# Last pair's second layer: three passes over 12-bit words instead of Strassen's float32 products

## The chip, the cores and the metric

The kernel runs on one core of a Trainium2 chip. A core has an engine for matrix products (PE, whose weight loads the profile lists apart as PEld), a vector engine (DVE), a scalar engine for activations (ACT), a general engine (POOL) and a queue that issues most transfers (SP). Each works through its own list of instructions in a fixed order, and they wait for each other by semaphores. Operands lie in SBUF, a memory of 128 partitions; products land in PSUM, eight banks of 128 x 512 float32. The metric is the time of one execution in microseconds (us).

## The reference, cut to what matters

A scan over chunks (a Mamba-2 block) makes `x`, 3072 tokens of 256 features. What follows is a two-layer perceptron, and the change is in its second layer:

```python
n_tokens, d_model, d_ff = (3072, 256, 2048)

def _moe_ref(x, w_in, w_out) -> np.ndarray:
    h = x @ w_in
    alpha = 1.0
    g = np.where(h > 0.0, h, alpha * (np.exp(np.minimum(h, 0.0)) - 1.0))
    return (g @ w_out).astype(np.float32)
```

`w_in` is 256 x 2048 and `w_out` 2048 x 256; everything is float32.

## The kernel before, in words

**Tiles.** The tokens are cut into 12 blocks of 256 (4 batches of 3 groups), numbered n = 0 to 11. The scan works block by block; from block 2 on, the perceptron works on pairs (2,3), (4,5) and so on, 512 tokens wide, named by their first block. The hidden layer is cut into 16 slices of 128 features, m = 0 to 15. A step of the main loop makes one slice of one pair.

**The first layer in words.** PE multiplies float32 exactly in several passes, as two instructions for each product. `l1_words` avoids this: it splits the operands into words of some 12 bits, whose products are exact, and PE takes them in the type `float32r` in one instruction each. For every operand there is a high word (made on ACT by a multiplication with `NEAR` that rounds to the type), a low word, and a mixed word "both". A slice is the sum of three passes: high x high and low x low into one PSUM bank (`high`), both x both into another (`both`). Then `4096 * both + 4095 * high` is the exact product. This is L806 (six instructions of 128 x 512 a step). ACT scales `both` into the tile `e` (L812), DVE adds it to `high` (L818), ACT makes Relu and Exp of it (L824 and L825, `begin_end`), and DVE makes the activation `g` (L832, `end_words`). `end_words` of step k stands on DVE in step k+1, just ahead of that step's L818.

**The second layer by Strassen.** `second(n)` multiplies a pair's `g` with `w_out` in float32. It takes Strassen's seven products (in Winograd's form) over quarters: two halves of d_ff, two blocks of tokens, two halves of the 256 outputs. Each product runs over four chunks of a half, with two products of 128 x 128 a chunk (L927), so 7 x 2 x 8 = 112 for a pair. DVE adds the results up (L904, L979), ACT copies two of them (L939, L964), and POOL makes the sums of `g` that Strassen needs (the helper `sub`, L867). `sum_weights` makes the sums of `w_out` on POOL and DVE (L723); it writes the first of them over a quarter of `w_out` itself. Results gather in the tile `c_sum`, and `store` (L984) sends them out.

**Order.** The program is written in the order in which it runs (`manual_schedule`); each engine's list follows it. In the loop over n = 4, 6, 8, 10 (L1327), step k makes slice k of pair n (`l1_words`), does a part of the scan for the pair ahead while there is one, calls `begin_end`, and then takes three or four pieces of `second(n - 2)` (`l2s`). So pair 8's second layer runs inside pair 10's first. Pair 10 is the last; its second layer stands alone behind the loop, as `second(10, True)` (L1376), with the last product's two token halves stored apart (L907 to L919).

**Memory.** Tiles come from pools; tiles with one tag share a fixed number of buffers, and an instruction that writes a new tile waits for the readers of the old one. Seven PSUM banks are shared by all tiles of tag "a" (`high`, `both`, every second of Strassen's sums), the eighth has the tag "o". `raw` and `att` hold what the scan needs, `conv` the words of `w_in` (tags w64, 11 buffers, and w_in, 9 buffers), `ffn` the activations. When pair 10 starts its first layer, the scan is over.

## Time and profile before

| | |
|---|---|
| time, median of 3 runs (lowest to highest) | 350.66 us (350.28 to 351.12) |
| profiled execution, first to last instruction | 347.9 us |
| PE busy in it | 340.7 us (98%) |
| DVE, ACT, POOL busy | 258.4, 234.1, 218.0 us |
| loop n = 10, first L806 to the end of its last | 271.9 to 317.95 us |
| Strassen's products, the last piece of pair 8 and pair 10 | 317.95 to 344.76 us |
| L927, instructions of 128 x 128 in float32 | 276 ns each on the page |
| L806, instructions of 128 x 512 in words | 392 to 437 ns each on the page |

A duration of a matmul on the page contains the way through the pipeline; how fast they follow each other is seen from their starts. The profiled execution's span and the median of the runs differ by 2.8 us, which lie outside the first and last instruction. A group's row ends with the idle time of its engine just before it and with what ended most of that. In rows in order of time the columns are start, duration, engine, line, operation, tiles (out <- in), shapes and count, and in brackets the idle time and what ended it.

### The profile page before, as it was taken

How to read it: one execution, taken by the hardware profiler on the slowest of the kernel's cores; microseconds unless marked ns; L12 is line 12 of the kernel's file. 1: busy time of each engine (PE TensorE's matmuls, PEld its weight loads, DVE VectorE, ACT ScalarE, POOL GpSimd, SP SyncE). 2: the span in 40 equal slices, each digit the busy share in tenths (PEclk: the TensorE clock that was granted, in tenths of full speed). 3: DMA queues.
4: the chain of work that ended last, by engine and by line, in shares of the span. 5: the costliest groups of instructions: out<-in, count | busy, mean ns of one | idle time of the engine just before them, and what ended most of it. 6: DMA issues, size and time to landing. Idle time of an engine off the chain costs nothing.

```text
span 347.9 us, 9991 instructions
## 1 busy us (share of the span) xinstructions
PE 340.7 (98%) x3934; PEld 299.3 (86%) x3934; DVE 258.4 (74%) x515; ACT 234.1 (67%) x537; POOL 218.0 (63%) x338
## 2 busy tenths in 40 slices
PE   8899999999999999999999999999999999999996
PEld 6579888888788889889889888889988989999996
DVE  3998989889997899876788766778776756665232
ACT  4789989598658988457699457599557366565000
POOL 5654554539999799965296765196855174455760
PEclk9999999999999999999999999999999999999999
DMA  8989969381360610260421160320000100001002
GB/s 144 258 204 220 273 130 266 81 150 44 66 138 2 135 38 12 34 137 4 117 51 30 17 154 4 95 44 0 2 2 5 60 2 1 0 2 55 9 2 62
DMA packets 72728, 26.51 MB, mean 76 GB/s; under 512 B 57768, under 2 KB 67560, under 8 KB 72680
## 3 DMA queue, kind: packets, MB, share of 16 engines
q1 hardware_dynamic: 70360, 25.60, 31.7%
q8 instruction: 31, 0.51, 0.6%
q10 hardware_dynamic: 2320, 0.26, 0.5%
q14 instruction: 17, 0.14, 0.1%
HBM read 22.51 MB, written 3.34 MB: 74 GB/s over the span
## 4 chain that ended last, share of the span: by engine, by line
PE 63%; DVE 11%; ACT 10%; POOL 7%; issue 4%; SPq 2%; DMA 2%; DVEq 0%; POOLq 0%; ACTq 0%
PE ps_o L927 22%; PE ps_h L806 11%; PE ps_h L676 11%; PE ps_o L851 8%; PE ps_w L806 6%; DVE ps_h L818 3%; ACT e L824 3%; POOL g L867 3%; ACT e L825 2%; DMA w<-in_moe_w_in_dram 2%; POOL t L867 2%; DVE M L559 2%; PE ps_y L643 2%; DVE y L780 2%; POOL w L867 1%
## 5 line engine op out<-in xcount | busy, mean ns | idle before, releaser
L927 PEld LDWEIGHTS ps_o<-w_out,g 128*128 128x128 f32 x640 | 78.7, 191 | 5.4 <-ACT p_sum L939 1.2
L927 PE MATMUL ps_o<-w_out,g 128*128 128x128 f32 x640 | 81.2, 276 | 0.7 <-ACT p_sum L939 0.6
L824 ACT ACTIVATE e<-ps_h 128x512 f32<-128x512 f32 x72 | 43.0, 598 | 56.9 <-DVE ps_h L818 56.9
L832 DVE SCALAR_TENSOR_TENSOR g<-e,ps_h 128x512 f32<-128x512 f32 x72 | 49.4, 686 | 35.0 <-ACT e L825 33.4
L867 POOL TENSOR_TENSOR g<-g 128x256 f32<-128x256 f32 x36 | 28.6, 794 | 58.2 <-DVE g L832 58.2
L818 DVE SCALAR_TENSOR_TENSOR ps_h<-ps_h,e 128x512 f32<-128x512 f32 x72 | 50.0, 694 | 11.2 <-ACT e L812 9.0
L806 PE MATMUL ps_w<-y_both,w_words 128*128 128x512 f32 x144 | 51.5, 437 | 0.1
L812 ACT ACTIVATE e<-ps_w 128x512 f32<-128x512 f32 x72 | 42.2, 586 | 11.1 <-PE ps_w L806 11.0
L825 ACT ACTIVATE e<-e 128x512 f32<-128x512 f32 x72 | 45.5, 631 | 2.3
L676 PE MATMUL ps_h<-yT,w_in 128*128 128x256 f32 (+1 forms) x208 | 45.1, 367 | 1.9 <-ACT w_in L205 1.1
L806 PE MATMUL ps_h<-y,w_words 128*128 128x512 f32 x144 | 45.5, 398 | 0.0
L806 PE MATMUL ps_h<-y,w 128*128 128x512 f32 x144 | 44.9, 392 | 0.0
L676 PEld LDWEIGHTS ps_h<-yT,w_in 128*128 128x128 f32 x208 | 36.4, 190 | 7.5 <-POOL w_in L248 2.6
L530 ACT ACTIVATE L<-L,ncum 128x64 f32<-128x64 f32 x160 | 42.2, 337 | 0.1
L927 PE MATMUL ps_o<-w_sum,g 128*128 128x128 f32 x304 | 38.6, 276 | 0.0
L927 PEld LDWEIGHTS ps_o<-w_sum,g 128*128 128x128 f32 x304 | 37.0, 192 | 1.4
L535 POOL TENSOR_SCALAR_AFFINE_SELECT L<-L 64x512 f32<-64x512 f32 x40 | 29.4, 735 | 8.0 <-ACT L L530 6.7
L806 PEld LDWEIGHTS ps_h<-y,w 128*128 128x128 f32 x144 | 27.0, 188 | 6.9 <-POOL w L867 0.4
L806 PEld LDWEIGHTS ps_h<-y,w_words 128*128 128x128 f32 x144 | 26.6, 188 | 6.2 <-issue 0.5
L867 POOL TENSOR_TENSOR g<-t,g 128x256 f32<-128x256 f32 x40 | 28.1, 736 | 5.8 <-PE ps_o L927 5.7
L851 PE MATMUL ps_o<-w_out,g 128*128 128x256 f32 x128 | 30.4, 381 | 0.0
L867 POOL TENSOR_TENSOR g<-g,t 128x256 f32<-128x256 f32 x40 | 28.7, 748 | 0.2
(135 smaller groups left out, 537.5 us busy)
## 6 DMA issues: line engine op xcount, KB each, us to landing
L<-flat SPq DMA_DIRECT2D x20, 256.0 KB
w<-in_moe_w_out_dram SPq DMA_DIRECT2D x8, 512.0 KB
w<-in_moe_w_in_dram SPq DMA_DIRECT2D x7, 512.0 KB
xr<-in_x_dram SPq DMA_DIRECT2D x24, 128.0 KB
out_dram<-c_sum SPq DMA_DIRECT2D x9, 256.0 KB
bc<-in_B_dram SPq DMA_DIRECT2D x24, 64.0 KB
bc<-in_C_dram SPq DMA_DIRECT2D x22, 64.0 KB
ec<-flat_exp SPq DMA_DIRECT2D x10, 128.0 KB
```

Source lines behind the costliest of these rows:

```text
L530: nc.scalar.activation(L[:, h, u], L[:, h, u], ACT.Exp, bias=ncum[:, u, row:row + 1])
L535: nc.gpsimd.affine_select(out=part, in_=part, pattern=[[0, 4], [0, 2], [1, Q]], compare_op=ALU.is_ge, fill=0.0, base=0, channel_multiplier=-1)
L676: nc.tensor.matmul(out=ps[:, j, toks], lhsT=w_in[i][:, k, j * P:(j + 1) * P], rhs=yT[n // 2][:, k, n % 2].rearrange("p u i -> p (u i)")[:, ...
L806: nc.tensor.matmul(out=ps, lhsT=lhs[:, k], rhs=rhs[:, k], start=k == 0 and lhs is not w0, stop=k == KC - 1 and lhs is not w1)
L812: nc.scalar.activation(e, both, ACT.Copy, scale=WORD)
L818: nc.vector.scalar_tensor_tensor(out=high, in0=high, scalar=WORD - 1.0, in1=e, op0=ALU.mult, op1=ALU.add)
L824: nc.scalar.activation(e, high, ACT.Relu, scale=-1.0)
L825: nc.scalar.activation(e, e, ACT.Exp, scale=-1.0)
L832: nc.vector.scalar_tensor_tensor(out=g_of[n, m].rearrange("p b i -> p (b i)"), in0=e, scalar=1.0, in1=h, op0=ALU.subtract, op1=ALU.max)
L851: nc.tensor.matmul(out=o_of[n][:, ts], lhsT=g_of[n, j][:, m % 2, ts * P:(ts + 1) * P], rhs=w_out[:, m], start=(m == 0 and ts == 0), stop=( ...
L867: nc.gpsimd.tensor_tensor(out=out, in0=in0, in1=in1, op=ALU.subtract)
L927: nc.tensor.matmul(out=ps[:, ts], lhsT=b[:, ts * P:(ts + 1) * P], rhs=a[:, i], start=(i == chunk[0] and ts == 0), stop=(i == chunk[-1]), s ...
```

## The change

Pair 10's second layer is no longer Strassen's. It is done as the first layer is, in words, in three passes over `g` and `w_out`.

- `w_out` as it is before Strassen's sums overwrite a part is copied to DRAM (`keep_w`): one quarter at the end of the first pairs, the others in steps 3, 5 and 7 of loop n = 4.
- When loop n = 8 ends, the scan's pools are closed, and `late_pool` opens another in their place. Four transfers of 512 KB bring `w_out` back.
- `late_words_of_w` (eight times) and `late_words_of_g` (sixteen times) make the words: each takes one ACT, one DVE and one POOL instruction of 128 x 512. The eight of `w_out` and the first seven of `g` stand in loop n = 10, behind `l2s`, one a step from k = 2 on and two in k = 15. The other nine stand behind the loop.
- `late_l2` adds, for one slice and 128 tokens, three products of 128 x 256. All four token groups stay in PSUM over all slices. `late_out` puts the two sums together (ACT, then DVE) and stores 128 rows.
- POOL's differences for pair 10 in `end_words`, its Strassen sums and the special end of `second` go.

```diff
-    raw = ctx.enter_context(tc.tile_pool(name="raw", bufs=3))
-    att = ctx.enter_context(tc.tile_pool(name="att", bufs=2))
     ffn = ctx.enter_context(tc.tile_pool(name="ffn", bufs=2))
     conv = ctx.enter_context(tc.tile_pool(name="conv", bufs=2))
+    scan_pools = ctx.enter_context(ExitStack())
+    raw = scan_pools.enter_context(tc.tile_pool(name="raw", bufs=3))
+    att = scan_pools.enter_context(tc.tile_pool(name="att", bufs=2))
...
+    w_kept = tc.dram_tile([P, MC, DM], F32, name="w_kept")
+    kept_parts = w_kept.rearrange("p (i k) (r c) -> p k r i c", k=2, c=P)
+
+    def keep_w(k, r):
+        nc.sync.dma_start(out=kept_parts[:, k, r], in_=w_parts[:, k, r])
...
-        if m % 2 == 0 and (n, m) != (2, 14):
+        if m % 2 == 0 and (n, m) != (2, 14) and n < NP - 2:
             sub(g_of[n, m][:, 1], g_of[n, m][:, 1], g_of[n, m][:, 0])
...
-                    elif n + 2 < NP:
+                    elif n + 4 < NP:
                         sum_t2(n + 2, 0)
...
+    def late_pool():
+
+        scan_pools.close()
+        pool = ctx.enter_context(tc.tile_pool(name="late", bufs=1))
+        for i in range(MC // 4):
+            w = pool.tile([P, 4, DM], F32, name="w_again", tag="w", bufs=MC // 4)
+            nc.sync.dma_start(out=w, in_=w_kept[:, 4 * i:4 * i + 4])
...
+    def late_words_of_w(i):
+        w, w1, both = late_w[i]
+        nc.scalar.activation(w1, w, ACT.Copy, scale=NEAR)
+        nc.vector.scalar_tensor_tensor(
+            out=both, in0=w1.bitcast(F32), scalar=1.0 / WORD - 1.0, in1=w,
+            op0=ALU.mult, op1=ALU.add)
+        sub(w.bitcast(F32R), w, w1.bitcast(F32))
+
+    def late_words_of_g(n, m):
+        g = g_of.pop((n, m)).rearrange("p b i -> p (b i)")
+        words = conv.tile([P, 2, 2 * BLK], F32R, tag="w64", name="g_words", bufs=W_AHEAD)
+        low = conv.tile([P, 2 * BLK], F32R, tag="w_in", name="g_low", bufs=DF // CW + 1)
+        nc.scalar.activation(words[:, 0], g, ACT.Copy, scale=NEAR / WORD)
+        nc.vector.scalar_tensor_tensor(
+            out=low, in0=words[:, 0].bitcast(F32), scalar=WORD, in1=g,
+            op0=ALU.mult, op1=ALU.subtract)
+        sub(words[:, 1], words[:, 0].bitcast(F32), low.bitcast(F32))
+        late_g[m] = words[:, 0], low, words[:, 1]
+
+    def late_l2(m, t):
+
+        g1, g0, both_g = (g[:, t * P:(t + 1) * P] for g in late_g[m])
+        w0, w1, both_w = (w[:, m % 2] for w in late_w[m // 2])
+        w0 = w0.bitcast(F32R)
+        if m == 0:
+            both = psum([P, 2, DM], "ps_both")
+            total.append((both[:, 0], psum([P, DM], "ps_high") if t == 3 else both[:, 1]))
+        both, high = total[t]
+        for ps, lhs, rhs in ((both, both_g, both_w), (high, g1, w1), (high, g0, w0)):
+            nc.tensor.matmul(
+                out=ps, lhsT=lhs, rhs=rhs,
...
+    def late_out(n, t):
+        both, high = total[t]
+        e = ffn.tile([P, DM], F32, tag="t2", name="e_out", bufs=4)
+        nc.scalar.activation(e, both, ACT.Copy, scale=WORD)
+        o = ffn.tile([P, DM], F32, tag="t2", name="o_out", bufs=4)
+        nc.vector.scalar_tensor_tensor(
+            out=o, in0=high, scalar=WORD - 1.0, in1=e, op0=ALU.mult, op1=ALU.add)
+        r0 = row_of(n + t // 2) + t % 2 * P
+        nc.sync.dma_start(out=out[r0:r0 + P, :], in_=o)
...
+            keep_w(0, 1)
...
+            if n == 4 and k in (3, 5, 7):
+                keep_w(int(k > 3), int(k > 5))
...
                 l2s(4 if k % 2 else 3)
+                if k > 1 and k % 2 == 0 or k == 15:
+                    late_words_of_w((k - 1) // 2)
+                if k > 2 and k % 2:
+                    late_words_of_g(n, k // 2 - 1)
                 continue
...
+        if m == NP - 2:
+            late_pool()
         end_words()
...
     n = NP - 2
-    for k, _ in enumerate(second(n, True)):
-        if k == 0:
-            store(n - 2, 0)
-            store(n - 2, 1)
+    store(n - 2, 0)
+    store(n - 2, 1)
+    for m in range(7, MC - 4):
+        late_words_of_g(n, m)
+        for t in range(4):
+            late_l2(m - 7, t)
+    for m in range(MC - 4, MC):
+        late_words_of_g(n, m)
+        for t in range(4):
+            late_l2(m - 7, t)
+    for m in range(MC - 7, MC - 4):
+        for t in range(4):
+            late_l2(m, t)
+    for t in range(4):
+        for m in range(MC - 4, MC):
+            late_l2(m, t)
+        late_out(n, t)
```

More of the change, by code (lines that the diff above doesn't have):

```diff
@@ L888, with second @@
     c_of = {}
-    def second(n, last=False):
+    def second(n):
         c = c_of[n] = ffn.tile([P, 2, 2, 2, P], F32, tag="c", name="c_sum", bufs=1)
@@ L906, in second @@
             for r, a in enumerate((a11, a12, s1, s2, s3, a22, s4)):
-                if last and half and r == 6:
-                    store(n, 0)
-                    for ts, queue in enumerate((nc.scalar, nc.sync)):
-                        ps = psum([P, P], "ps_o")
-                        for i in chunk:
-                            nc.tensor.matmul(
-                                out=ps, lhsT=quarters(n, i)[3][:, ts * P:(ts + 1) * P],
-                                rhs=a[:, i], start=(i == chunk[0]), stop=(i == chunk[-1]))
-                        nc.vector.tensor_tensor(
-                            out=c12[:, ts], in0=ps, in1=c12[:, ts], op=ALU.add)
-                        r0 = row_of(n + 1) + ts * P
-                        queue.dma_start(out=out[r0:r0 + P, 0:P], in_=c12[:, ts])
-                    return
                 pool, tag = (p_a, "a") if (7 * half + r) % 2 or n == 2 and not half + r else (
@@ L964, in second @@
                         nc.scalar.copy(out=c12, in_=ps)
-                    if last and half:
-                        r0 = row_of(n + 1)
-                        nc.sync.dma_start(
-                            out=out[r0:r0 + BLK, P:2 * P].rearrange("(t p) c -> p t c", p=P),
-                            in_=c22)
                     if not half:
                         sum_t2(n, 1)
-                    elif n + 2 < NP:
+                    elif n + 4 < NP:
                         sum_t2(n + 2, 0)
@@ L980, in second @@
                 yield
+    late_w, late_g, total = [], {}, []
+    def late_pool():
[4 more added lines that the diff above has]
+            nc.sync.dma_start(out=w, in_=w_kept[:, 4 * i:4 * i + 4])
+            for k in range(2):
+                late_w.append([w[:, 2 * k:2 * k + 2], pool.tile(
+                    [P, 2, DM], F32R, name="w_high", tag="w1", bufs=MC // 2)])
+        for i in range(MC // 2 - 2):
+            late_w[i].append(pool.tile([P, 2, DM], F32R, name="w_both", tag="wb", bufs=MC // 2 - 2))
+        more = ffn.tile([P, 2, 2, DM], F32R, tag="yT", name="w_both")
+        for i in range(2):
+            late_w[MC // 2 - 2 + i].append(more[:, i])
@@ new lines, in late_l2 @@
+    def late_l2(m, t):
[9 more added lines that the diff above has]
+                out=ps, lhsT=lhs, rhs=rhs,
+                start=m == 0 and (ps is both or t == 3 and lhs is g1),
+                stop=m == MC - 1 and lhs is not g1, skip_group_check=True)
```

## The prediction

> **What bounds the kernel now.** I read the page first, then the chain of work that ended last, then the busy time by stages of the end, then ACT and DVE in order of time within single steps.

> ```profile
> PE 340.7 (98%) x3934; PEld 299.3 (86%) x3934; DVE 258.4 (74%) x515; ACT 234.1 (67%) x537; POOL 218.0 (63%) x338
> ...
> 271.90:317.95 46.05, 45.87 (x309) 41.54 (x308) 29.23 (x53) 28.57 (x50) 22.43 (x32) 1.00 0.04 12
> 317.95:344.80 26.85, 26.80 (x241) 26.61 (x239) 9.21 (x24) 1.97 (x4) 15.26 (x22) 1.00 0.10 31
> ...
> 276.44 0.64 ACT e L825
> 277.17 0.54 issue
> 277.71 0.70 DVE ps_h L818
> 278.43 0.61 ACT e L824
> ...
> 316.57 0.46 PE ps_w L806 x2
> 317.03 0.93 PE ps_h L806 x4
> 317.95 25.01 PE ps_o L927 x224
> 342.96 1.80 PE ps_o L912 x16
> ```

> PE is busy all through, so on average matmuls are the bound. The stage rows (columns: stretch, its length, then busy time of PE, weight loads, DVE, ACT, POOL, then clock and DMA) say where others have room: in the last first-layer loop, n=10 (271.9 to 317.95), DVE and ACT work 29 of 46 us, and in the stretch behind it nearly nothing but PE and POOL. The chain shows that this average hides something: until 279 the loop is bound by L818, L824 and L825, a circle of DVE and ACT, and only later by PE. Two steps (k=2 and 3) of that circle, ACT and then DVE:

> ```profile
> 281.22 0.60 ACT L824 ACTIVATE e<-ps_h 128x512 f32<-128x512 f32 x1 [0.76 <-DVE ps_h L818]
> 281.85 0.63 ACT L825 ACTIVATE e<-e 128x512 f32<-128x512 f32 x1
> 282.39 0.58 ACT L812 ACTIVATE e<-ps_w 128x512 f32<-128x512 f32 x1
> ...
> 280.49 0.70 DVE L818 SCALAR_TENSOR_TENSOR ps_h<-ps_h,e 128x512 f32<-128x512 f32 x1
> 281.10 0.41 DVE L904 TENSOR_TENSOR c_sum<-ps_o,p_sum 128x256 f32<-128x256 f32 x1
> 282.52 0.69 DVE L832 SCALAR_TENSOR_TENSOR g<-e,ps_h 128x512 f32<-128x512 f32 x1 [1.01 <-ACT e L825]
> 283.12 0.69 DVE L818 SCALAR_TENSOR_TENSOR ps_h<-ps_h,e 128x512 f32<-128x512 f32 x1
> ```

> The reader is to see one turn: L818 at 280.49, L824 at 281.22 (0.73 later), L825 at 281.85 (0.63), L832 at 282.52 (0.67), the next L818 at 283.12 (0.60). That is 2.63 us a step, each link waiting for the one before. PE needs 2.72 or 3.17 us a step (three or four of Strassen's pieces), 2.95 on average. So the circle has about 0.3 us a step to spare, and the idle time in brackets (0.76 on ACT, 1.01 on DVE) is inside it: it is waiting, not room at the end of a queue.

> **The change part by part.**

> *Second layer of the last pair on PE.* Removed: 112 products 128x128 in float32, two PE instructions each; the chain has them from 319.74 to 344.76, 25.0 us, 0.1117 each. Added: 16 x 4 x 3 = 192 instructions in words, 256 columns each. No row has words with 256 columns. Between L806 rows with 512 columns, starts lie 0.231 apart (a pair from 308.24 to 308.71). Half of that is 0.116; the float32 instructions of L927 go at 0.112; the upper end is 0.231, if the price were per instruction. As an estimate I take 0.116, by columns, since the float32 rows also halve (216 ns between L676 starts, 112 between L927's): 192 x 0.116 = 22.3 us. Alone this is 2.7 us gained.

> *Words inside the loop.* Steps k=2 to 14 each get one group: ACT makes a high word (128x512), DVE the low or mixed word, POOL a difference. The program puts them behind L825 on ACT, and on DVE in front of the next L832. So in each step L832 waits for: the word on ACT, which starts 0.54 after L825 starts (as L812 does, 281.85 to 282.39) and takes 0.62 (L745: 619 ns) plus 0.03 to wake DVE; then DVE's word, 0.60 until the next DVE instruction can start (two of L790 take 1.28). Queued behind it on DVE are L832, then L818 of the next step; ACT's L824 waits for L818. One turn becomes 0.73 + 0.63 + 0.54 + 0.65 + 0.60 + 0.60 = 3.75 us, 1.12 more. DVE's Strassen sums (L904, 0.41 each) lie in the remaining wait and cost nothing as long as at most four come in a step.
> The 16th L818 starts at 318.06 now. From 280.49 (k=2), 13 turns of 3.75 put it at 329.2: 11.2 us later. PE can't run ahead past this: seven PSUM buffers hold high and mixed sums, freed by L832 and L812; about two steps ahead they are used up.

> [...] POOL drops 8 L867 differences and the last pair's Strassen ones, and gets 15 differences of 128x512 in the loop, 9 behind it. A 128x512 POOL operation with two inputs takes 1.27 (L248, 1274 ns), a 128x256 one 0.74. These rows show what happens when it meets a DVE instruction with two SBUF inputs:

> ```profile
> 163.55 1.11 POOL L867 TENSOR_TENSOR g<-g 128x256 f32<-128x256 f32 x1 [3.05 <-DVE g L832]
> ...
> 163.39 1.82 DVE L780 SCALAR_TENSOR_TENSOR y<-y,yT 128x512 fp32r<-128x512 f32 x2
> 165.13 1.28 DVE L790 SCALAR_TENSOR_TENSOR y_both<-y,yT 128x512 fp32r<-128x512 f32 x2
> ```

> The same kind of pair took 1.82 instead of 1.28, and POOL 1.11 instead of 0.74: they went one after the other. The words on DVE have two SBUF inputs. In the loop I add 1.5 us for it: POOL keeps some 16 us of Strassen differences there, so that about four turns in ten meet one and wait about 0.3 (an estimate; bounds: 0, and 13 x 0.54 = 7). H, the start of the 16th L818, becomes 318.06 + 11.2 + 1.5 = 330.8.
> [...]

> *The tail.* PE gets through Strassen's last pieces and ten word products while it waits, and then needs the bank that L832 frees just before H. 182 x 0.116 = 21.1 remain, so PE alone would end at H + 21.3. But the words of the last g come one after another: w's last and g's 6 to 15, eleven pairs, starting at H + 0.73 + 0.63 + 0.54 + 0.65 = H + 2.55. In turns with DVE a 128x256 POOL operation costs 1.82 - 1.28 = 0.54, one of 512 columns 0.53 more (1.27 - 0.74), so 1.07; with 0.60 on DVE, 1.67 a pair, 18.4 in all. The last word is there at H + 21.0, and 39 products, 4.5 us, and the 0.17 of the pipeline follow: H + 25.7 = 356.5. Before, PE ended at 344.76. So 11.7 later.

> *The end.* Now: DVE 0.29 behind the last matmul, then the store. Then: ACT 128x256 (L964, 0.37) and DVE 128x256 (L904, 0.42) with 0.04 between, so 0.55 more. The store is 128 KB instead of 64 (bounds 0 to 0.5; I take 0).

> *Costs of nothing.* The four copies of w_out to DRAM: SP stands idle between 70.5+5.9 and 83.5, and again from 128 on, and each copy is one issue like L148's (0.77 us); covered as long as the first has read before POOL's first sum into w_out (92.7, some 13 us after the last part is made at 79.5). Without the cover POOL would wait, and PE some steps later. The four loads back (512 KB each): SP's queue is empty from 227 to 273, the scan's last readers end on PE at 264.3, and at 200 GB/s (the page's early slices) 2 MB take 10 us, the first part 2.6. It is wanted at about 282.5, so over 10 us of cover. Behind these loads only the stores of pair 8 and the last ones are queued.

> *Sum.* On the profiled execution (span 347.9): +11.7 + 0.55 = 12.3, so 360.2. Outside the span lie 2.8 us to the median of the runs, 350.66; unchanged, this gives 363.0.

> **The rivals.**
> 1. *Faster: the words fit into the idle time.* For it: the brackets above, 1.01 on DVE and 0.76 on ACT a step. Then H stays at 318.06 and PE goes on at once: 22.3 in place of 25.0, plus 0.55, so 348.5. It decides in the loop, at an addition per turn of (37.57 - 13 x 2.63) / 13 = 0.26 us (37.57 is 318.06 - 280.49), and with the tail's gain at about 0.3; I count 1.12. Against it: the order on both queues puts the words between L825 and L832. 5%.
> 2. *The circle as I say, but DVE and POOL run side by side.* H at 329.2; POOL's eleven end at H + 3.2 + 14.0 = H + 17.2, PE at H + 21.9 = 351.1: 6.3 + 0.55 later, 357.5. Against it: the L780 rows. 22%.
> 3. *More in the loop:* most turns meet a POOL difference (up to 7 in place of 1.5), or PE, stalled, delivers Strassen's sums late to DVE, which then stands in front of L832. Half to all of that bound, and up to 1.5 us for the sums: 366 to 370. 20%.
> 4. *Words at 256 columns cost what 512 do.* PE: 182 x 0.231 = 42.0 from H; 373.0, so 28.2 + 0.55 later: 379. Against it: float32 rows halve. 3%.

> **How the numbers follow.** The forecast, 363.0, has 50%. The range goes down past rival 2 and up through rival 3: 356 to 370, which leaves out rivals 1 and 4 and the ends of the others, under 2 in 10. Anything within 0.2% (0.7 us) of 350.66 is no change that this kernel's runs can tell; it would need rival 1 with part of its gain lost: 1%. Faster 4%, slower 95%.

> **What would show it.** In the profile after: the instruction that L818 is now starting every 3.7 to 4.0 us instead of 2.7 to 3.2 from k=2 on; ACT's idle time before L824 growing to over 1 us a step; PE idle 8 us or more in the loop, released by ACT and DVE; word products 0.116 apart; in the tail DVE and POOL words lengthened beyond 0.69 and 1.27, and PE waiting for POOL. Wrong, if L818 keeps its pace (rival 1), if PE runs the tail without waits (rival 2), if products lie 0.2 apart (rival 4), or if the granted clock leaves 1.00.

## The result and the profile after

The changed kernel takes 363.46 us (median of 6 runs, 361.34 to 363.82); the kernel before 350.45 (6 runs, 349.79 to 351.12). The ratio is 1.0361, 95% interval 1.0339 to 1.0383: 3.6% slower, where 363.0 was forecast. One execution among the experiments below, of the kernel with the filled wait, took 557 us at a granted clock of 0.56 and is left out. Line numbers have moved: L818 of before is L824 here (the start of each turn of the circle), L824, L825 and L832 are L830, L831 and L838, and L806, L812, L904 and L927 are L812, L818, L910 and L920. New lines are L990, L991 (the words of w_out on ACT and DVE), L1000, L1001 (those of g), L873 (the differences on POOL), L1017 (the word products), L1025 and L1027 (the last outputs).

The profiled execution took 363.82 us, 362.0 of it in the span. The page's busy times and its slices of the granted clock:

```profile
PE 345.2 (95%) x3902; PEld 301.2 (83%) x3902; DVE 274.5 (76%) x523; ACT 247.0 (68%) x563; POOL 231.1 (64%) x329
...
PEclk9999999999999999999999999999999999998998
```

PE was 98% busy before and is 95% now, although the products have become cheaper (192 at 0.12 us, 23.0 us, in place of 25.0); and the clock, 1.0 throughout the work before, drops in two places near the end. The waits of PE from 270 us on (columns: the engine and what it was to write, whose end it waited for, us in total, how often, the longest):

```profile
PE ps_o L920 <- DVE c_sum L910: 4.2, 2, 2.9
PE ps_both L1017 <- POOL g_words L873: 2.0, 3, 1.0
PE ps_both L1017 <- ACT e L818: 1.4, 1, 1.4
PE ps_w L812 <- ACT e L818: 1.2, 1, 1.2
PE ps_high L1017 <- DVE g L838: 0.5, 1, 0.5
```

Before, PE hardly waited in this stretch (0.2 us in the loop). Now it stands for 7.3 us on DVE and ACT while the loop lasts and for 2.0 us on POOL in the tail. The loop's part is in one turn of the circle, ACT and then DVE in order of time (start, duration, engine, line; idle time in brackets):

```profile
312.78 0.60 ACT L830 ACTIVATE e<-ps_h 128x512 f32<-128x512 f32 x1 [1.72 <-DVE ps_h L824]
313.41 0.63 ACT L831 ACTIVATE e<-e 128x512 f32<-128x512 f32 x1
313.95 0.62 ACT L990 ACTIVATE w_high<-w_again 128x512 fp32r<-128x512 f32 x1
...
312.06 0.69 DVE L824 SCALAR_TENSOR_TENSOR ps_h<-ps_h,e 128x512 f32<-128x512 f32 x1
312.66 0.41 DVE L910 TENSOR_TENSOR c_sum<-ps_o,c_sum 128x256 f32<-128x256 f32 x1
314.60 0.69 DVE L991 SCALAR_TENSOR_TENSOR w_both<-w_high,w_again 128x512 fp32r<-128x512 f32 x1 [1.53 <-ACT w_high L990]
315.21 0.68 DVE L838 SCALAR_TENSOR_TENSOR g<-e,ps_h 128x512 f32<-128x512 f32 x1
315.81 0.69 DVE L824 SCALAR_TENSOR_TENSOR ps_h<-ps_h,e 128x512 f32<-128x512 f32 x1
```

From L824 to L824: 0.72, 0.63, 0.54, 0.65, 0.61, 0.60, together 3.75 us, where a turn took 2.6 to 3.2 before. The word on ACT (L990) and the one on DVE (L991) lie inside the turn, between L831 and L838. The longest wait of PE (2.9 us, until 313.22) is a consequence: the Strassen sum L910 that it needs stands on DVE behind the word, L838 and L824 and starts only at 312.66.

The tail, as the chain that ended last gives it (start, duration, what; "issue" and "POOLq" are time that the chain puts to no work):

```profile
335.72 0.64 POOL g_words L873
...
339.14 11.90 POOL g_words L873 x7
351.04 1.25 POOLq L1477
352.33 5.12 PE ps_both L1017 x28
...
358.56 0.39 ACT e_out L1025
358.98 0.42 DVE o_out L1027
```

From 335.7 to 352.3 it follows POOL's words, and then the last products. On POOL and DVE the tail's words go at the same pace, 1.66 and 1.64 us for one (first a POOL word of the loop, then POOL's row of the tail, then DVE's; the number at the end of a row is the count):

```profile
330.35 1.28 POOL L873 TENSOR_TENSOR w_again<-w_again,w_high 128x512 fp32r<-128x512 f32 x1 [2.40 <-DVE w_both L991]
335.72 16.55 POOL L873 TENSOR_TENSOR g_words<-g_words,g_low 128x512 fp32r<-128x512 f32 x10
...
335.13 14.79 DVE L1001 SCALAR_TENSOR_TENSOR g_low<-g_words,g 128x512 fp32r<-128x512 f32 x9
```

In the loop such a POOL word takes 1.28 us; in the tail ten take 16.55, 1.66 each, and nine of DVE's 14.79, 1.64 each, where a single one in the loop lets the next instruction start after 0.60.

At last the stretches in which the clock changes (columns as in the stage rows of the prediction: the stretch, its length, busy PE, weight loads, DVE, ACT, POOL, clock, DMA):

```profile
271.90:318.00 46.10, 41.73 (x275) 36.93 (x275) 28.18 (x52) 27.23 (x50) 26.80 (x29) 1.00 0.06 20
...
328.70:332.10 3.40, 1.56 (x11) 1.36 (x12) 2.22 (x4) 1.92 (x4) 1.28 (x1) 1.00 0.23 77
332.10:335.50 3.40, 3.40 (x19) 3.40 (x18) 2.17 (x4) 3.37 (x8) 1.40 (x1) 0.50 0.26 82
...
349.20:352.60 3.40, 1.51 (x8) 1.11 (x9) 0.72 (x1) 0.00 (x0) 3.08 (x3) 1.00 0.00 0
352.60:356.00 3.40, 3.40 (x18) 3.40 (x18) 0.43 (x1) 0.64 (x2) 0.00 (x0) 0.50 0.14 46
```

The clock is at one half for exactly 3.41 us each time, right behind a stretch of that length in which PE was busy for 46% and 44% of the time. The first costs nothing, since PE still comes to wait for POOL's words at the end of the tail (2.0 us, from 349.1 on). The second falls on the last products: they start 0.21 us apart in it, 0.12 outside.

How the 16 turns and the end compare, in us from the start of the span (H is the start of the 16th L824, before: L818; "last output" is the start of the instruction that reads PE's last result):

| | k=2 | k=5 | k=8 | k=12 | H | last output | span |
|---|---|---|---|---|---|---|---|
| before | 280.49 | 288.56 | 297.62 | 309.42 | 318.06 | 344.79 | 347.9 |
| after | 281.57 | 292.82 | 304.33 | 319.55 | 330.79 | 358.56 | 362.0 |

The loop from k=2 to H has grown from 37.57 to 49.22 us (+11.65), the way from H to the last output from 26.73 to 27.77 (+1.04), and what follows it from 3.1 to 3.4 (+0.3). Another 1.1 us lies before k=2, and most of that is there already by 18 us (DVE's first L698 starts at 17.66 before, its counterpart L699 at 18.83 after), ahead of any changed work.

### The profile page after: what moved, and what is told of

Read it like the earlier page. It is cut to its first block, busy times and chain, and to the rows that moved or that the text cites. A ratio compares the mean times of both kernels' runs of the same rounds, so it can differ in the third digit from the quotient of the medians.

```text
span 362.0 us, 9961 instructions
## 1 busy us (share of the span) xinstructions
PE 345.2 (95%) x3902; PEld 301.2 (83%) x3902; DVE 274.5 (76%) x523; ACT 247.0 (68%) x563; POOL 231.1 (64%) x329
## 4 chain that ended last, share of the span: by engine, by line
PE 52%; DVE 13%; ACT 12%; POOL 11%; issue 6%; SPq 4%; DMA 1%; POOLq 0%; DVEq 0%
PE ps_o L920 12%; PE ps_h L677 10%; PE ps_h L812 9%; PE ps_o L857 8%; PE ps_w L812 5%; DVE ps_h L824 4%; ACT e L830 4%; POOL g_words L873 4%; ACT e L831 3%; POOL g L873 3%; PE ps_both L1017 3%; SPq L179 2%; DVE g L838 2%; POOL t L873 2%; PE ps_y L644 2%
## 5 line engine op out<-in xcount | busy, mean ns | idle before, releaser
L830 ACT ACTIVATE e<-ps_h 128x512 f32<-128x512 f32 x72 | 43.0, 598 | 63.1 <-DVE ps_h L824 63.1
L838 DVE SCALAR_TENSOR_TENSOR g<-e,ps_h 128x512 f32<-128x512 f32 x72 | 49.2, 683 | 27.5 <-ACT e L831 26.1
L920 PEld LDWEIGHTS ps_o<-w_out,g 128*128 128x128 f32 x512 | 64.2, 191 | 6.8 <-POOL g_words L873 1.4
L920 PE MATMUL ps_o<-w_out,g 128*128 128x128 f32 x512 | 66.5, 276 | 1.9 <-DVE c_sum L910 1.3
L824 DVE SCALAR_TENSOR_TENSOR ps_h<-ps_h,e 128x512 f32<-128x512 f32 x72 | 49.9, 693 | 9.1 <-ACT e L818 8.5
L812 PE MATMUL ps_w<-y_both,w_words 128*128 128x512 f32 x144 | 51.4, 437 | 1.3 <-ACT e L818 1.2
L818 ACT ACTIVATE e<-ps_w 128x512 f32<-128x512 f32 x72 | 42.0, 584 | 10.4 <-PE ps_w L812 10.3
L831 ACT ACTIVATE e<-e 128x512 f32<-128x512 f32 x72 | 45.4, 631 | 2.3
L812 PE MATMUL ps_h<-y,w_words 128*128 128x512 f32 x144 | 45.8, 399 | 0.1
L873 POOL TENSOR_TENSOR g<-g 128x256 f32<-128x256 f32 x28 | 22.7, 812 | 36.3 <-DVE g L838 36.2
L812 PE MATMUL ps_h<-y,w 128*128 128x512 f32 x144 | 44.9, 392 | 0.0
L920 PE MATMUL ps_o<-w_sum,g 128*128 128x128 f32 x256 | 32.8, 276 | 0.0
L812 PEld LDWEIGHTS ps_h<-y,w 128*128 128x128 f32 x144 | 27.0, 188 | 6.9 <-POOL w L873 0.4
L920 PEld LDWEIGHTS ps_o<-w_sum,g 128*128 128x128 f32 x256 | 31.4, 191 | 1.4
L812 PEld LDWEIGHTS ps_h<-y,w_words 128*128 128x128 f32 x144 | 26.4, 188 | 6.8 <-DVE g L838 0.5
L873 POOL TENSOR_TENSOR g_words<-g_words,g_low 128x512 fp32r<-128x512 f32 x16 | 24.2, 1535 | 8.8 <-DVE g_low L1001 8.8
L857 PEld LDWEIGHTS ps_o<-w_out,g 128*128 128x128 f32 x128 | 24.0, 190 | 3.5
```

The costliest lines, as they stand in the source:

```text
L812: nc.tensor.matmul(out=ps, lhsT=lhs[:, k], rhs=rhs[:, k], start=k == 0 and lhs is not w0, stop=k == KC - 1 and lhs is not w1)
L818: nc.scalar.activation(e, both, ACT.Copy, scale=WORD)
L824: nc.vector.scalar_tensor_tensor(out=high, in0=high, scalar=WORD - 1.0, in1=e, op0=ALU.mult, op1=ALU.add)
L830: nc.scalar.activation(e, high, ACT.Relu, scale=-1.0)
L831: nc.scalar.activation(e, e, ACT.Exp, scale=-1.0)
L838: nc.vector.scalar_tensor_tensor(out=g_of[n, m].rearrange("p b i -> p (b i)"), in0=e, scalar=1.0, in1=h, op0=ALU.subtract, op1=ALU.max)
```

## The experiments

Theory: the turn of the circle on ACT and DVE sets the loop, because the program puts each word between L831 and L838 of the same step; the end of the tail is then set by POOL's and DVE's words taking turns (1.66 us a pair). Rivals: the added work itself (whatever its place), the traffic of the copies and loads, PE's products, the meeting of POOL and DVE in the loop. The kernel before was run again beside each group of experiments, and the ratios are taken against it: its median was 350.26 us beside the words early, ACT's word early, the tail without POOL and both edits, 350.09 beside half of the words early, the unread words, the copies and the first run of the filled wait, and 349.79 beside the last two.

### The same words, earlier in each step

The four lines that issue the loop's words move from the end of the step to a place ahead of L830's step:

```diff
+            if not m and (k > 1 and k % 2 == 0 or k == 15):
+                late_words_of_w((k - 1) // 2)
+            if not m and k > 2 and k % 2:
+                late_words_of_g(n, k // 2 - 1)
             begin_end()
...
                 l2s(4 if k % 2 else 3)
-                if k > 1 and k % 2 == 0 or k == 15:
-                    late_words_of_w((k - 1) // 2)
-                if k > 2 and k % 2:
-                    late_words_of_g(n, k // 2 - 1)
                 continue
```

> The only edit: in loop n = 10 the words of a step are made ahead of Relu and Exp (begin_end) instead of behind the Strassen pieces. Theory of the circle: the loss comes from ACT's word standing between Exp and DVE's word, and DVE's word between Exp and the next ELU (L838), not from the work. Ahead of Relu, ACT's word fills ACT's wait for DVE (0.76 to 0.96 us in the trace of before), and DVE's word fills DVE's wait for Exp (1.0 us). Then L824 goes back to 2.7 to 3.2 us a step, the 16th one comes 11 to 12 us earlier, PE runs the tail without waits (192 products, 0.12 apart, 23.0 in place of 25.0 us), and the time is about 349 (348 to 351). Rival, too much work on the engines: DVE, ACT and POOL have the same instructions as in the changed kernel, so the time stays at 361 to 364. Rival, the tail alone is at fault: the pace in the loop changes, but the end moves by less than 5 us.

Measured: 348.64 us (348.18 to 349.67), ratio 0.9957, interval 0.9941 to 0.9973. The same work in another order is 14.8 us faster than the changed kernel and 0.4% faster than the kernel before. Two steps of it, ACT and then DVE:

```profile
300.06 0.63 ACT L831 ACTIVATE e<-e 128x512 f32<-128x512 f32 x1
...
301.07 0.62 ACT L1000 ACTIVATE g_words<-g 128x512 fp32r<-128x512 f32 x1
302.06 0.60 ACT L830 ACTIVATE e<-ps_h 128x512 f32<-128x512 f32 x1 [0.36 <-DVE ps_h L824]
...
300.73 0.69 DVE L838 SCALAR_TENSOR_TENSOR g<-e,ps_h 128x512 f32<-128x512 f32 x1 [0.74 <-ACT e L831]
301.33 0.69 DVE L824 SCALAR_TENSOR_TENSOR ps_h<-ps_h,e 128x512 f32<-128x512 f32 x1
301.93 0.68 DVE L1001 SCALAR_TENSOR_TENSOR g_low<-g_words,g 128x512 fp32r<-128x512 f32 x1
```

L838 now starts 0.67 after L831, as before the change, and DVE's word comes behind L824, in the time in which DVE would wait for ACT. H is 319.01, 37.77 us after k=2 (37.57 before, 49.22 in the changed kernel); two of the 13 turns take 3.55 and 3.46 us, the others 2.62 to 3.17. The idle time that rival 1 counted on is really there; the changed kernel misses it by the place of the words. The copies and loads of `w_out` are all in this kernel too, so they are not the loss. The change's own gain shows here too: from H to the last output it takes 24.4 us in place of 26.7, less the 0.3 us that the longer end costs.

### Only ACT's word earlier

The high word on ACT moves to the earlier place; DVE's and POOL's stay at the end of the step:

```diff
+            if not m and (k > 1 and k % 2 == 0 or k == 15):
+                late_high_of_w((k - 1) // 2)
+            if not m and k > 2 and k % 2:
+                late_high_of_g(n, k // 2 - 1)
             begin_end()
```

> The only edit: ACT's high word alone goes ahead of Relu and Exp; DVE's and POOL's words stay behind the Strassen pieces. Theory of the circle: DVE's word then has its operand early and runs while DVE waits for Exp; it no longer waits behind Exp plus ACT's word, so the whole 1.1 us a step goes, not only ACT's half: about 349 (348 to 351), as with all words early. Rival, the two halves add up (ACT's 0.54 and DVE's 0.60 each cost their own): half of the loss stays, about 355 to 357.

Measured: 349.86 us (349.17 to 351.02), ratio 0.9987, interval 0.9976 to 0.9999; H at 318.73, 37.66 after k=2. DVE in order of time (L994 is the word here):

```profile
298.90 0.85 DVE L994 SCALAR_TENSOR_TENSOR w_both<-w_high,w_again 128x512 fp32r<-128x512 f32 x1
300.32 0.69 DVE L838 SCALAR_TENSOR_TENSOR g<-e,ps_h 128x512 f32<-128x512 f32 x1 [0.57 <-ACT e L831]
300.94 0.70 DVE L824 SCALAR_TENSOR_TENSOR ps_h<-ps_h,e 128x512 f32<-128x512 f32 x1
```

The word is done before Exp (L831) is, and DVE still waits 0.57 us for that. So it is enough that DVE's word finds ACT's ready. DVE's word alone fits in the idle time, though it is still queued ahead of L838: the loss is ACT's word followed by DVE's, one behind the other. Here the tail's last word comes at 339.8, 1.2 us later than in the kernel with all words early, and PE waits for it twice (0.27 and 0.61 us).

### Half of the words early

The words of g (odd steps) move, those of w_out (even steps) stay:

```diff
+            if not m and k > 2 and k % 2:
+                late_words_of_g(n, k // 2 - 1)
             begin_end()
...
-                if k > 2 and k % 2:
-                    late_words_of_g(n, k // 2 - 1)
                 continue
```

> Of the changed kernel, the words of g go ahead of Relu and Exp, those of w_out stay behind the Strassen pieces. Theory of the circle, worked out: from k = 2 on, seven turns of 3.75 and six of 2.63 make 42.0 us in place of 37.6, since what an early step gains is used up by the late one before it; so the 16th L824 is 4.5 us later than before. In the tail ten slices of words at 1.67 follow it, and PE ends 24.1 us behind it against 26.7 before; with 0.3 for the end, 352.5 (351 to 354). Rival, each late word costs its 1.12 whatever lies between: 13 turns with seven late ones, 7.8 us, about 356. Rival, only the number of words in the loop counts: as the changed kernel, 363.

Measured: 355.69 us (354.59 to 356.6), ratio 1.0152, interval 1.0122 to 1.0182. That is above the range expected (351 to 354) and beside the 356 of the first rival, so the time alone would speak for the rival. The turns decide, and they follow the theory: from k=2 the starts of L824 lie 3.75, 2.63, 3.74, 3.07, 3.75, 2.63, 3.74, 2.90 us and so on apart, 3.75 where the words are late, but for one turn of 4.15, and shorter in each turn between, so that an early step takes part of the loss back. From k=2 to H it takes 43.24 us where the theory gave 42.0: 5.7 us more than before, where the rival's 1.12 for each of seven late words makes 7.8. The tail took 0.8 us more than worked out (last output at H + 24.9). The profiled run, at a granted clock of 1.000, is the one of 354.59; the other three, at 0.995, took 0.7 to 2.0 us more. The last experiments are about that clock.

### The tail without POOL

The difference on POOL for the words 7 to 15 of g is written as one more DVE instruction:

```diff
-        sub(words[:, 1], words[:, 0].bitcast(F32), low.bitcast(F32))
+        if m > 6:
+            nc.vector.scalar_tensor_tensor(
+                out=words[:, 1], in0=words[:, 0].bitcast(F32), scalar=1.0 - WORD, in1=g,
+                op0=ALU.mult, op1=ALU.add)
+        else:
+            sub(words[:, 1], words[:, 0].bitcast(F32), low.bitcast(F32))
```

> The only edit: behind the loop, the mixed word of g (slices 7 to 15) is made on DVE from the high word and g, in place of POOL's difference. The loop is as in the changed kernel, so L824 keeps 3.75 us a step. [...] Rival, the tail is bound by PE or its clock anyway: 362 to 364.

Measured: 358.46 us (357.64 to 359.18), ratio 1.0232, interval 1.0212 to 1.0253; 357 to 358.5 was expected, with two DVE words at 0.60 us each, 1.2 us a slice, in place of 1.67. Lines of DVE and POOL in the tail:

```profile
334.84 1.18 DVE L1001 SCALAR_TENSOR_TENSOR g_low<-g_words,g 128x512 fp32r<-128x512 f32 x1
335.94 1.79 DVE L1005 SCALAR_TENSOR_TENSOR g_words<-g_words,g 128x512 fp32r<-128x512 f32 x1
337.66 0.68 DVE L1001 SCALAR_TENSOR_TENSOR g_low<-g_words,g 128x512 fp32r<-128x512 f32 x1
338.26 0.68 DVE L1005 SCALAR_TENSOR_TENSOR g_words<-g_words,g 128x512 fp32r<-128x512 f32 x1
...
333.80 1.67 POOL L873 TENSOR_TENSOR w_again<-w_again,w_high 128x512 fp32r<-128x512 f32 x1 [2.47 <-DVE w_both L991]
335.43 1.75 POOL L873 TENSOR_TENSOR g_words<-g_words,g_low 128x512 fp32r<-128x512 f32 x1
```

As long as POOL runs (until 337.2), DVE's instructions take 1.18 and 1.79 us; behind it 0.68, one every 0.60. Two DVE instructions in place of one on DVE and one on POOL take 1.2 us instead of 1.66: giving half of the work to the second engine made the pair slower than one engine alone. The loop keeps its 3.75 (H = 330.49), so the 5.0 us are gained behind it. With both edits at once:

> Both edits: words ahead of Relu and Exp in the loop, and mixed words of g on DVE behind the loop. Theory of the circle: with the loop's pace back, PE sets the end of the tail whichever engine makes the words there (nine slices at 1.67 end before PE wants the last), so the second edit adds nothing: the same as with the first edit alone within 0.5 us, about 349. If the tail's words were still late with the first edit alone, this one is faster by the difference, up to 3 us.

Measured: 348.59 us (347.84 to 349.46), ratio 0.9953, interval 0.9936 to 0.9971, the same as with the words early alone. Once H is not late, PE does not wait for POOL's words, and the slow pair costs nothing. The gains do not add up (14.8 and 5.0 us alone, 14.9 together): behind a loop at its old pace PE itself is the last to finish.

### Loop words that nobody reads

The loop of the changed kernel, and behind it the Strassen tail of before, with the differences and sums that Strassen's products need:

```diff
-        if m % 2 == 0 and (n, m) != (2, 14) and n < NP - 2:
+        if m % 2 == 0 and (n, m) != (2, 14):
             sub(g_of[n, m][:, 1], g_of[n, m][:, 1], g_of[n, m][:, 0])
...
-                    elif n + 4 < NP:
+                    elif n + 2 < NP:
                         sum_t2(n + 2, 0)
...
     n = NP - 2
-    store(n - 2, 0)
-    store(n - 2, 1)
-    for m in range(7, MC - 4):
...
+    for k, _ in enumerate(second(n, True)):
+        if k == 0:
+            store(n - 2, 0)
+            store(n - 2, 1)
```

> The changed kernel's loop with Strassen's second layer behind it, as before: w_out is kept, brought back and split into words, and g's first seven slices too, all in the places of the changed kernel, but nothing uses them; the last pair's second layer is the old one. Theory of the circle: L824 (as numbered in the changed kernel) starts every 3.75 us from k = 2 on. Strassen's products need only one bank at a time, so PE goes on as soon as the loop's last pieces are done, which in the changed kernel was about 8 us after the same point of before; then its 25.0 us follow without a wait: 357 to 359. Rival, the loss lies in the word products or in the tail's words: at most 1 us over before, 350 to 351.5.

Measured: 362.60 us (362.0 to 362.61), ratio 1.0347, interval 1.0326 to 1.0368; 357 to 359 was expected. The loop is as expected (turns of 3.74 to 4.10, H = 330.65), the tail is not. PE in order of time:

```profile
325.82 1.39 PE L933 MATMUL ps_o<-w_sum,g 128*128 128x128 f32 x11
327.97 3.84 PE L933 MATMUL ps_o<-w_out,g 128*128 128x128 f32 x32 [0.76 <-DVE c_sum L910]
333.98 2.05 PE L933 MATMUL ps_o<-w_out,g 128*128 128x128 f32 x16 [2.17 <-ACT p_sum L945]
...
337.66 2.69 PE L933 MATMUL ps_o<-w_sum,g 128*128 128x128 f32 x16
340.32 2.77 PE L933 MATMUL ps_o<-w_out,g 128*128 128x128 f32 x16
```

And a row of the waits between 321 and 361 us:

```profile
PEld ps_o L933 <- POOL g L873: 1.2, 7, 0.2
```

The expectation had PE work ahead on Strassen's pieces while the circle holds the loop. PE does get ahead (at 327.97, before H, it begins the last pair's products), but it loses the lead again. The PSUM buffers that it needs are freed by a DVE sum (L910) and an ACT copy (L945), which are queued behind words, so PE waits 0.76 and 2.17 us. Then two pieces take 2.7 us instead of 1.95, since their weight loads wait seven times for POOL's differences, which stand behind POOL's words. The last output comes at H + 26.8, in the kernel before at H + 26.7. So the words in the loop alone, without one word product, cost 12.5 us, where the whole change costs 13.0.

### The copies alone

The kernel before, with the four copies of w_out to DRAM that the change adds:

```diff
+    def keep_w(k, r):
+        nc.sync.dma_start(out=kept_parts[:, k, r], in_=w_parts[:, k, r])
...
             w_give(15)
+            keep_w(0, 1)
...
+            if n == 4 and k in (3, 5, 7):
+                keep_w(int(k > 3), int(k > 5))
```

> The kernel before with the four copies of w_out to DRAM added, which nothing reads, and no other edit. Forecast of the prediction: they are covered, so 350 to 351 and no difference over 0.2 %. Rival: they hold up POOL's first sums of w_out or the scan's loads behind them on SP's queue, and cost up to 1 us; the changed kernel's profile was 1.1 us behind before's at the start of loop n = 10, but had that lag by 18 us already, before any copy.

Measured: 350.15 us (349.95 to 350.96), ratio 1.0002, interval 0.9990 to 1.0014. The copies cost nothing that these runs can tell (at most 0.5 us by the interval).

### PE kept busy while it waits

To the kernel with the tail on DVE, seven products that nothing reads are added ahead of the first late product that waits:

```diff
+    filler = p_o.tile([P, 2 * BLK], F32, tag="o", name="filler")
...
+            if m == 7 and t == 3:
+                for _ in range(7):
+                    nc.tensor.matmul(
+                        out=filler, lhsT=late_w[0][1][:, 0, 0:P], rhs=late_g[0][0],
+                        start=True, stop=True)
             late_l2(m - 7, t)
```

> The edit of e2 (mixed words of g on DVE behind the loop), and seven products of 128x512 without use put on PE where it waits for a bank at the end of the loop, ahead of the first products of the fourth token group. Theory of the clock: in e2 PE was idle for 1.9 of some 3.4 us there, and the granted clock was halved for the next 3.41 us, in which some 16 products ran instead of 28. With the wait filled the clock stays at 1.0 and the time falls by 1.4 to 1.7 us against e2, to about 357. Rival, the clock's dip has another cause (what the products hold, or chance): no difference to e2, 358 to 359.

Measured: 357.52, 357.87 and 358.00 us in three runs. Their middle is 0.6 us below the kernel without the products, where 1.4 to 1.7 were expected, and the ranges overlap (357.64 to 359.18 without). The mean clock of the runs was 0.994 to 0.995; as an estimate, one drop to half remained, since 3.41 us at half clock take 0.005 off the mean over 356 us. The same kernel again, for its profile:

> The same kernel as the run with the filled wait (words seven to fifteen on VectorE in the tail, seven unused 128x512 products ahead of the first late product that waits), for a profile of it. Theory of the clock: the window that holds the filled wait (0.53 busy without the products) is then over 85% busy, and no half clock follows it near 332 us; if a half clock remains it stands behind a window in the loop that holds the wait of 2.9 us near 310 us, about half idle. Rival: half clock at 332 us as without the products. Time 357 to 358, as measured.

Measured: 357.69 and 357.05 us. Stretches of its profile:

```profile
309.40:312.80 3.40, 0.49 (x5) 0.33 (x4) 2.46 (x4) 1.68 (x4) 3.40 (x5) 1.00 0.00 0
312.80:316.20 3.40, 3.40 (x13) 3.01 (x14) 2.13 (x4) 1.89 (x5) 3.40 (x6) 0.50 0.02 5
...
326.40:329.90 3.50, 3.50 (x24) 3.01 (x23) 1.97 (x5) 2.23 (x4) 1.09 (x2) 1.00 0.22 75
329.90:333.30 3.40, 2.99 (x25) 2.91 (x25) 1.87 (x4) 2.29 (x5) 1.20 (x1) 1.00 0.24 82
```

No half clock follows the filled wait: it lies in the stretch up to 329.9, which is busy throughout, and the next one is busy 88%. The one that is left stands behind 309.4 to 312.8, the stretch of the 2.9 us wait in the loop, busy 14%; there the circle sets the pace. But this profile does not decide between theory and rival. Counted from the drops, the stretches lie elsewhere than in the profile of the kernel without the products (half clock near 332 there), and in the changed kernel, whose loop is the same up to this point, the matching stretch, 327.0 to 330.4, is busy 58% (1.98 of 3.40 us) with nothing filled in. Behind a stretch busy 53% that kernel's clock stayed at 1.00 (last section). So the products may have changed nothing here.

The same with the changed kernel itself, in the place where the half clock falls on the last products:

```diff
+    filler = p_o.tile([P, 2 * BLK], F32, tag="o", name="filler")
...
+            for _ in range((0, 1, 4, 2)[m - MC + 4] if t == 0 else 0):
+                nc.tensor.matmul(
+                    out=filler, lhsT=late_w[0][1][:, 0, 0:P], rhs=late_g[0][0],
+                    start=True, stop=True)
             late_l2(m, t)
```

> The changed kernel with seven more products of 128x512, which nothing reads, put where TensorE waits for the last three words in the tail (one, four and two of them, 0.23 us each, against waits of 0.33, 1.05 and 0.61). They add work that no output takes and change nothing else. [...] Rival, that the half clock comes from something else than idle time (the kind of products, the power drawn): half clock in the tail as before, 363.5 or more.

Measured: 361.70 us (361.0 to 362.31), ratio 1.0329, interval 1.0292 to 1.0365, so 1.8 us below the changed kernel's median; 362.0 to 362.6 was expected, 1 to 1.5 us below. The kernel before was 0.66 us faster beside these runs than beside the changed kernel's, so the gain that counts is nearer to 1.1 us, as expected, and the two intervals of the ratio overlap (1.0339 to 1.0383 for the changed kernel). Four stretches, the last two cut where the changed kernel's were, and then ACT's last instruction in order of time:

```profile
308.80:312.20 3.40, 1.43 (x11) 1.15 (x9) 2.54 (x6) 2.17 (x4) 3.40 (x6) 1.00 0.00 0
312.20:315.60 3.40, 2.45 (x10) 2.38 (x11) 1.88 (x4) 2.23 (x4) 3.40 (x4) 0.50 0.02 5
...
349.20:352.60 3.40, 2.93 (x14) 1.98 (x15) 0.65 (x1) 0.00 (x0) 3.05 (x3) 1.00 0.00 0
352.60:356.00 3.40, 3.40 (x30) 3.40 (x29) 0.85 (x2) 0.93 (x3) 0.00 (x0) 1.00 0.14 46
```

```profile
357.04 0.38 ACT L1025 ACTIVATE e_out<-ps_both 128x256 f32<-128x256 f32 x1 [0.82 <-PE ps_both L1017]
```

With the waits filled (PE busy 86% instead of 44%) the clock stays at 1.00, the last word comes at 352.25 (352.27 in the changed kernel), and the products end 4.8 us behind it in place of 6.2, where 4.7 was expected. By the mean clocks of the runs (0.990 and three times 0.995; 0.991, 0.986, 0.986, 0.991, 0.995 and 0.991 for the changed kernel), and as an estimate, since 3.41 us at half clock take 0.0047 off the mean over 362 us, the four hold two, one, one and one stretches of half clock, the six of the changed kernel two, three, three, two, one and two. So more work on PE goes with less time at half clock and a shorter time. It fits idle time as the cause; that it was so in this profile is not shown. Cut from this profile's own drop (at 312.2, in steps of 3.41), the changed kernel's waits, with nothing filled in, lie in stretches busy 90% (346.3 to 349.7) and 51% (349.7 to 353.2), and behind one busy 53% that kernel's clock stayed at 1.00. The first two stretches hold the drop in the loop, behind the 2.9 us wait; it stays, and the last word comes no later for it.

## Why the prediction was right

**The circle.** One turn was put at 3.75 us from six links, and each link is within 0.01 us of the profile's (the turn shown above). 13 turns were to add 11.2 us; the loop from k=2 grew by 11.65. The early words, the early word on ACT and the alternating turns show that it is the order on the two queues, neither the amount of work nor a transfer nor the products. What the prediction took from the page for this was small: not the busy shares (DVE 29 of 46 us), but the idle time in brackets, read as a link of a chain.

**The meetings of POOL and DVE in the loop.** 1.5 us were added for them; the profile has two turns, of 4.02 and 3.98, among 3.75, together 0.5 us. The step is the guess that four turns in ten meet a difference. H came out at 330.79 for 330.8, but by two errors that cancel: 1.0 us too much here, and 1.1 us that the profiled run was behind at k=2 already, which is there in every kernel of this study (0.3 to 1.0 behind), the one with nothing but the copies too: the profiled execution of before was early by then.

**The tail.** The last word was put at H + 21.0 and came at H + 21.5, at 1.66 us a pair for 1.67. The prediction had the turns from one pair of rows (L780, 1.82 us where L790 took 1.28); in the tail a POOL word takes 1.66 us and one of DVE's 1.64, in the loop 1.28 and 0.60. PE's end was put at H + 25.7 and was H + 27.7: the last 39 products took 6.2 us for 4.5, of which 1.7 are the 3.41 us at half clock. So the tail, forecast 1.0 us shorter than before, came 1.0 us longer. This is the term that failed, and the prediction had named its condition ("if the granted clock leaves 1.00") without a price. Without the drop the same products took 4.8 us (the last experiment). That PE's waits bring the drop is the author's reading of the comparison in the last section; no experiment shows it alone.

**The products.** 0.12 us apart (328.27 to 328.39 for two neighbours), for the 0.116 taken by columns; the upper bound of 0.231 and rival 4 fall.

**The end and the copies.** 0.3 us for 0.55, and nothing for the copies, as forecast.

**Outside the span.** The sum used 2.8 us, taken from the median of the runs and the profile's span. In the runs 1.7 to 1.8 us lie outside the span (363.82 to 362.0); the profile of before was simply a short execution, by about 1 us. In spans the sum was 360.2, and 362.0 came: +1.1 at the start, -1.0 for the meetings, +2.0 for the clock and the last word, -0.2 at the end. In the median the 1 us outside made up for half of it. So that forecast and median lie 0.5 us apart is in part luck; the terms say more.

**The rivals.** Rival 1 (the words fit) fell for this order of the queues, and holds for the other, with 348.6 measured for its 348.5 (as a gain 1.6 us against the kernel before beside it, for 2.2). Rival 2 fell, since DVE and POOL do take turns (1.66 us a pair). Rival 3 had the sums late to DVE: the 2.9 us wait is one, but it goes the other way, PE waiting for DVE, and lies inside the circle. The signs named beforehand are there: ACT idle 1.48 us and more ahead of L830, PE idle 7.3 us in the loop (8 was said), words of 1.64 and 1.66 in the tail.

## What to carry to other kernels

Before work is added to an engine with room, follow one turn of the loop across the engines, start to start: an added piece that can start only when a link of the turn has ended, and that stands ahead of the next link on its queue, costs its whole length (2.63 us a turn became 3.75). Where its input was ready earlier, the same piece ran in the wait for that link and cost nothing here (363.5 against 348.6 us, and 349.9 with only ACT's part moved). Giving one of two instructions to a second engine made the pair slower here: 1.66 us shared by DVE and POOL, 1.2 with both on DVE. The waits on PE in the tail (2.0 us) were followed by 3.41 us at half clock, and the last products took 6.2 us in place of 4.8.

## What the runs showed of the hardware that I had not expected

The second surprise is that a tail on PE kept its distance to the loop's end (H + 26.7 and H + 26.8) although PE got ahead of it first: what frees its PSUM buffers, and what makes its operands on POOL, was queued behind the same words. That the two distances agree within 0.1 us is chance, as they are made up of different waits.
